# Local-plus-block attention and an MLP on one core: fewer early loads, key copies on chip, and a new order list

## The chip, the cores and the metric

The kernel runs on one core of one Trainium2 chip. The metric is the device time of one execution in microseconds, smaller being better. Names used below: PE is TensorE (matmuls and transposes), DVE is VectorE, ACT is ScalarE, POOL is GpSimd, SP is SyncE, which here only issues loads and stores. SBUF is the on-chip memory of 128 rows, PSUM the memory into which PE writes.

## The reference

Four batches of eight heads, 768 tokens, head width 64. Each query sees the keys within 15 tokens of it, and beside them 24 summaries of the sequence, one for each block of 32 tokens: the key of a block is the maximum over its keys, its value the mean of its values. The attention output goes into a two-layer MLP with a rational activation. q, k and v are 32-bit, the weights come as 64-bit floats.

```python
k_sum = k.reshape(B, H, nb, block, D).max(axis=3)
v_sum = v.reshape(B, H, nb, block, D).mean(axis=3)
scores_l = scale * np.matmul(q, k.transpose(0, 1, 3, 2))
mask_l = np.abs(pos[:, None] - pos[None, :]) < window      # window = 16
scores_s = scale * np.einsum('bhsd,bhnd->bhsn', q, k_sum) + np.log(block)
scores_all = concat([where(mask_l, scores_l, -1e9), scores_s])
a = softmax(scores_all)
attn = a @ concat([v, v_sum])                              # 3072 tokens x 512
h = attn @ w_in                                            # 512 -> 2048
P = a[0] + a[1]*h + a[2]*h**2 + a[3]*h**3
Q = 1.0 + abs(b[0])*abs(h) + abs(b[1])*h**2
out = (P / (Q + 1e-6)) @ w_out                             # 2048 -> 512
```

## The kernel before

**Units of work.** The 3072 tokens are cut into 48 "halves" of 64 queries (`HQ`), 12 in a batch, all eight heads at once. A half needs 96 keys and values around its queries (`NKW`, 16 tokens of margin on either side) and the 24 block summaries, so 120 columns (`NK`). Eight halves make a group of 512 tokens, and there are six groups. For each group the MLP runs over 16 column blocks of 128 (`fc`), so 96 steps; a step n is written g_fc, h0_4 being step 4. In a step the first layer (`moe1`) gives h from x, which is kept as a high part xh and a rest xl; the activation (`gelu`, parts a to k) gives a high part gh and a rest gl; and the second layer (`moe2`) adds into four PSUM tiles po. Each layer takes three products of high parts and rests.

**A half.** PE writes the scores (sc), DVE adds the mask and finds the row's extreme (sm), ACT takes the exponentials with their sum, DVE the reciprocal, POOL or DVE scales (ss). PE then transposes the result into pt, ACT copies it to pts, PE multiplies by the values (av), ACT copies av to xh, and DVE takes av minus xh as xl.

**Halves 0 to 7** ("early") are the first group. Their keys lie in `kres`, the padded keys of the whole first batch (four loads K0 to K3), and their queries in `qres`; each half has a value tile of its own (`vres`: vw0, vw1, vr0 to vr3, vlast). From half 8 on `att_load` brings queries (qw) and windowed keys (kw) of a half into two alternating buffers. The block means of the values come from PE: `window_average` and `value_average` add up averaging products of the value tiles in one PSUM tile (vf), and `first_means` copies the result into rows 96 to 119 of each value tile. The second batch's means (vf1, `quarter_average`) are made likewise.

**Weights.** `w_load` brings one column block of both weights as 1 MB of 64-bit numbers (wr). `w_split` turns them into a high part and a rest: a Prelu over them on ACT (called a prelude here), a scaling of one byte plane on POOL, a shift on DVE, then a copy to the high part on ACT (a cast) and the rest on DVE.

**What sets the order.** Up to about step 13 a list written out by hand, `TEXT` (lines 48 to 59). `token` (line 683) turns each entry into instructions, and each engine issues its own in the order in which the list names them. A letter is a kind of work, the number a half, a block or a step: K and k load and reduce keys, Q loads queries, M loads constants, V and v load and average values, F and G load more values of the first two batches, m copies the means, h takes a half one stage on, A is `att_load`, W and w load and split weights, x and y are the layers, g with a letter a part of the activation. Z is a spare matmul of the mask against the identity whose result nobody reads; `FILL` puts one such matmul ahead of half 8's transposes. The steps behind the list are ordered by a scheduler from a loop (lines 752 to 786), which the change leaves alone.

**PSUM.** Eight buffers: four (`ps_o`) for early scores and later po, two (`ps_h`) for h, for early pt and for the spares, two (`ps_a`) for vf, av and the scores and pt of halves 8 and up.

All engine instructions go through one wrapper, so the profile gives them all line 114; they are told apart by their tiles' names. In the order rows a name carries a running number, and wearly, w8 and so on are finished weights.

## Time and profile before

| | |
|---|---|
| times of three runs | 629.84 (median), 628.6, 635.0 us |
| the profiled execution | 629.4 us |
| its span in the trace | 627.5 us |
| mean granted clock of PE | 0.997 of full speed |
| PE busy | 615.8 us, 98% of the span |
| DVE, ACT, POOL busy | 558.9, 458.8, 261.4 us |

The span runs from the first to the last instruction of the trace; the 1.9 us that the execution took beyond it lie around it. Busy time is the time in which an engine worked on an instruction, waiting left out; PE's ends are modelled, since its matmuls overlap. An engine that is busy for 98% of the span leaves 11.7 us in which it did nothing.

### The profile page before, as it was taken

The numbers are of one execution on the slowest core, as the hardware profiler recorded it, in microseconds if no ns is written. First come the engines' busy times: TensorE is split into PE (matmuls) and PEld (weight loads), VectorE is DVE, ScalarE is ACT, GpSimd is POOL, SyncE is SP. The second block draws the span as 40 slices with busy tenths as digits, with TensorE's granted clock in tenths as the row PEclk, the third lists the DMA queues.
The fourth block names the chain that finished last, engine by engine and source line by source line (L and its number), as shares of the span: only waits on it lengthen the run. The fifth ranks groups of instructions, "written<-read, shape, count | busy, mean of one in ns | idle before, by whom it ended". The sixth has DMA issues, their size and how long they took to land.

```text
span 627.5 us, 11968 instructions
## 1 busy us (share of the span) xinstructions
PE 615.8 (98%) x4126; PEld 494.0 (79%) x4126; DVE 558.9 (89%) x1139; ACT 458.8 (73%) x1031; POOL 261.4 (42%) x351
## 2 busy tenths in 40 slices
PE   7989999999999999999999999999999999999997
PEld 4466777878888888888888888888888888888885
DVE  5889999999799999799999899888988988898885
ACT  3999999986866767866766867757767765755563
POOL 1587598725433435323334145334243242222221
PEclk9999999999999999999999999999999999999999
DMA  8989989232444444334434524224233120100001
GB/s 315 315 327 332 282 254 296 81 110 75 151 128 129 119 148 133 135 98 126 118 104 129 166 79 129 77 66 129 89 115 119 40 67 1 67 1 1 1 1 67
DMA packets 51444, 80.29 MB, mean 128 GB/s; under 512 B 6344, under 2 KB 32904, under 8 KB 49464
## 3 DMA queue, kind: packets, MB, share of 16 engines
q1 hardware_dynamic: 49672, 75.01, 36.6%
q0 software_dynamic: 1280, 4.39, 3.0%
q8 instruction: 32, 0.52, 0.3%
q14 instruction: 28, 0.23, 0.1%
q10 hardware_dynamic: 432, 0.13, 0.1%
HBM read 60.33 MB, written 14.75 MB: 120 GB/s over the span
## 4 chain that ended last, share of the span: by engine, by line
PE 90%; DMA 4%; ACT 2%; DVE 1%; POOL 1%; SPq 1%; issue 0%; ACTq 0%; POOLq 0%
PE po L114 42%; PE h L114 41%; PE av L114 4%; PE sc L114 3%; DMA wr<-in_wio_dram 2%; DMA vf<-in_vpad_dram 1%; DMA mask<-in_cmask_dram 1%; ACT ss L114 1%; POOL ss L114 1%; PE pt L114 1%; ACT wr L114 1%; SPq L114 1%; DVE wr L114 0%; ACT pts L114 0%; POOL wr L114 0%
## 5 line engine op out<-in xcount | busy, mean ns | idle before, releaser
L114 POOL TENSOR_TENSOR gl<-tu,ta 128x512 fp32r<-128x512 f32 x96 | 132.5, 1381 | 292.3 <-DVE tu L114 153.0
L114 PE MATMUL po<-wearly,gh 128*128 128x512 f32 x384 | 120.4, 395 | 0.0
L114 PE MATMUL po<-w,gh 128*128 128x512 f32 x384 | 119.7, 393 | 0.0
L114 ACT ACTIVATE ta<-tq,cs 128x512 f32<-128x512 f32 x96 | 69.7, 726 | 68.2 <-DVE tq L114 67.3
L114 POOL TENSOR_SCALAR ss<-ss,sm 128x120 f32<-128x120 f32 x176 | 85.3, 504 | 38.5 <-DVE sm L114 37.7
L114 PE MATMUL h<-xh,wearly 128*128 128x512 f32 x384 | 96.7, 392 | 0.1
L114 PE MATMUL h<-xh,w 128*128 128x512 f32 x384 | 96.7, 391 | 0.1
L114 PEld LDWEIGHTS h<-xh,wearly 128*128 128x128 f32 x384 | 71.6, 188 | 16.4 <-ACT pts L114 0.7
L114 PEld LDWEIGHTS h<-xh,w 128*128 128x128 f32 x384 | 71.8, 188 | 15.5 <-PE spare L114 0.6
L114 PEld LDWEIGHTS po<-wearly,gh 128*128 128x128 f32 x384 | 70.9, 188 | 16.1 <-issue 1.6
L114 PEld LDWEIGHTS po<-w,gh 128*128 128x128 f32 x384 | 71.3, 188 | 15.6 <-issue 1.1
L114 ACT ACTIVATE ss<-ss,sm 128x120 f32<-128x120 f32 x188 | 71.8, 386 | 13.7 <-DVE sm L114 13.7
L114 DVE SCALAR_TENSOR_TENSOR gh<-tu,cs,ta 128x512 fp32r<-128x512 f32 x96 | 74.2, 774 | 8.5 <-ACT ta L114 1.2
L114 DVE SCALAR_TENSOR_TENSOR tu<-tu,cs,tq 128x512 f32<-128x512 f32 x96 | 72.5, 755 | 2.9
L114 PE MATMUL po<-w,gl 128*128 128x512 f32 x192 | 74.9, 390 | 0.0
L114 PE MATMUL po<-wearly,gl 128*128 128x512 f32 x192 | 74.9, 390 | 0.0
L114 ACT ACTIVATE tu<-h,cs 128x512 f32<-128x512 f32 x96 | 74.6, 779 | 0.0
L114 DVE SCALAR_TENSOR_TENSOR tu<-tu,cs,h 128x512 f32<-128x512 f32 x96 | 71.4, 744 | 2.7
L114 DVE SCALAR_TENSOR_TENSOR tq<-tq,gh 128x512 f32<-128x512 f32 x96 | 67.4, 702 | 2.8
L114 ACT ACTIVATE ta<-h,cs 128x512 f32<-128x512 f32 x95 | 64.6, 679 | 0.5 <-POOL gl L114 0.2
L114 DVE TENSOR_TENSOR tu<-tu,h 128x512 f32<-128x512 f32 x96 | 64.9, 676 | 0.0
L114 ACT ACTIVATE ta<-ta 128x512 f32<-128x512 f32 x96 | 60.8, 633 | 2.5
(92 smaller groups left out, 905.1 us busy)
## 6 DMA issues: line engine op xcount, KB each, us to landing
wr<-in_wio_dram SPq DMA_DIRECT2D x15, 1024.0 KB, 6.8
cross<-tb SPq DMA_DIRECT2D x32, 256.0 KB, 2.0
vw<-in_vpad_dram SPq DMA_DIRECT2D x42, 192.0 KB, 3.4
kw<-in_kwin_dram SPq DMA_DIRECT2D x40, 192.0 KB, 3.8
pts<-cross SPq DMA_DIRECT2D x96, 64.0 KB, 2.0
out_dram<-o SPq DMA_DIRECT2D x23, 256.0 KB, 2.1
qw<-in_qw_dram SPq DMA_DIRECT2D x40, 128.0 KB, 3.0
kr<-in_kraw_dram SPq DMA_DIRECT2D x12, 384.0 KB, 8.4
```

The costliest lines, as they stand in the source:

```text
L114: out = getattr(self.engine, name)(*args, **kw)
```

## The change

1. The early halves' values load as 128 rows rather than 96. The last 32 rows are those that follow in memory; rows 96 to 119 are overwritten by the means before they are read.
2. The windowed keys of halves 8 to 11, which lie in the first batch, are no longer loaded. POOL copies them out of `kres` (token B), and `att_load` brings keys from the second batch on.
3. Masks (three of 120 columns), identity and averaging matrices came as three loads of 180, 64 and 139 KB. Now the middle mask, the identity and a narrower averaging matrix come as one load of 156 KB into a tile `both`, and POOL makes the masks of the first and last half of a batch from the middle one, by a copy and a memset each (token N).
4. The averaging products write only the 24 rows of PSUM that are used (`NKW:NK`) instead of 120, and the activation's coefficients are loaded straight into `cs`.
5. Spare matmuls have 312 columns instead of 360.
6. The list `TEXT` is new from the first entry to the last (583 entries instead of 578).

```diff
--- before.py
+++ after.py
@@ -45,20 +45,20 @@
-TEXT = ("K0 k0 K2 K1 S0 k1 k2 K3 k3 Q0 h2 h3 M0 h3 h3 h0 h1 h0 Q1 h3 h0 h0 h3 h3 h1 W0 M1 h3 Z4 F0 h2 h0 w0 w0 w0 h8 h3 h2 h1 h1 h1 h2 h6 h6 h6 h4 h5 h7 h7 h7 h0 V2 v2 w0 w0 h6 h14 v9 "
...
-AVGW = NK + NB - 8
-AVGH = NK + NB - 2
+TEXT = ("K2 K0 Q0 S0 k0 k2 K1 k1 K3 k3 B8 h8 M0 W0 h0 N0 h0 h2 Q1 h1 h1 h3 h0 h0 h0 w0 V2 F0 h3 h3 h1 h1 Z1 V3 V5 B9 h3 Z0 h6 h1 v2 w0 h7 h7 h7 h7 V6 h2 h3 h2 h2 v9 h4 h5 h0 w0 h7 w0 "
...
+AVGH = 40
+NCONST = NK + P + AVGH + NB
...
@@ -125,26 +125,24 @@
-    ident = const.tile([P, P], F32, name="ident")
-    mask = const.tile([P, 3, NK], F32, name="mask")
-    coef = const.tile([P, 6], F32, name="coef")
+    both = const.tile([P, NCONST + 2 * NK], F32, name="both")
+    mid, ident, avg = both[:, 0:NK], both[:, NK:NK + P], both[:, NK + P:NCONST]
+    ends = both[:, NCONST:].rearrange("p (m k) -> p m k", m=2)
...
-    vw = [const.tile([NK, DM], F32, name=f"vw{i}") for i in range(2)]
+    vw = [const.tile([P, DM], F32, name=f"vw{i}") for i in range(2)]
...
-    kfull = wm.tile([P, NPAIR * SPAD + AVGW + AVGH], F32, tag="wm", name="kres")
-    kres = kfull[:, 0:NPAIR * SPAD].rearrange("p (r s) -> p r s", r=NPAIR)
-    avg = kfull[:, NPAIR * SPAD:]
-    avgw = kfull[0:NKW, NPAIR * SPAD + AVGW:]
+    kfull = wm.tile([P, NPAIR * SPAD], F32, tag="wm", name="kres")
+    kres = kfull.rearrange("p (r s) -> p r s", r=NPAIR)
     def setup():
-        nc.scalar.dma_start(out=coef[:, 0:4], in_=a)
-        nc.scalar.dma_start(out=coef[:, 4:6], in_=b)
-        dve.tensor_scalar_mul(cs[:, 0:6], coef, SH)
+        nc.scalar.dma_start(out=cs[:, 0:4], in_=a)
+        nc.scalar.dma_start(out=cs[:, 4:6], in_=b)
+        dve.tensor_scalar_mul(cs[:, 0:6], cs[:, 0:6], SH)
...
@@ -204,11 +202,12 @@
     def value_average(kind, av, n, k, vt):
...
-        pe.matmul(av[:NK, :], avg[:, AVGW - NK - 8 * (k // 2):AVGW - 8 * (k // 2)], vt, start=(order[kind] == 1), stop=(order[kind] == n))
+        lo = NB - 8 - 8 * (k // 2)
+        pe.matmul(av[NKW:NK, :], avg[:, lo:lo + NB], vt, start=(order[kind] == 1), stop=(order[kind] == n))
     def quarter_average(av, n, k, vt):
...
-        lo = NKW + NB - 8 - 8 * (k // 2)
+        lo = NB - 8 - 8 * (k // 2)
...
@@ -216,7 +215,8 @@
     def window_average(av, n, jj):
...
-        pe.matmul(av[:NK, :], avgw[:, AVGH - NK - 2 * jj:AVGH - 2 * jj], vres[jj][0:NKW, :], start=(order["v"] == 1), stop=(order["v"] == n))
+        lo = AVGH - 2 * jj
+        pe.matmul(av[NKW:NK, :], avg[0:NKW, lo:lo + NB], vres[jj][0:NKW, :], start=(order["v"] == 1), stop=(order["v"] == n))
     def first_means(av):
...
@@ -241,7 +241,8 @@
...
-        syn.dma_start(out=kw[jj % 2][:, 0:NKC - 1], in_=kwin[bi, j])
+        if bi:
+            syn.dma_start(out=kw[jj % 2][:, 0:NKC - 1], in_=kwin[bi, j])
     def key_blocks(jj):
...
@@ -291,7 +292,7 @@
     def softmax(jj, sc):
...
-        mt = mask[:, 0 if j == 0 else (2 if j == NJ - 1 else 1), :]
+        mt = ends[:, 0, :] if j == 0 else ends[:, 1, :] if j == NJ - 1 else mid
...
@@ -360,7 +361,8 @@
...
-        syn.dma_start(out=vt[0:NKW, :], in_=vpad[bi, j * HQ:j * HQ + NKW, :])
+        rows = P if jj < HPG else NKW
+        syn.dma_start(out=vt[0:rows, :], in_=vpad[bi, j * HQ:j * HQ + rows, :])
...
@@ -374,7 +376,7 @@
     def turned(jj, early=False):
...
-            pe.matmul(pt[:, 0:3 * NK], ident, mask.rearrange("p m k -> p (m k)"), start=True, stop=True)
+            pe.matmul(pt[:, 0:NCONST], ident, both[:, 0:NCONST], start=True, stop=True)
...
@@ -649,8 +651,8 @@
...
-    vres = vw + [mp.tile([NK, DM], F32, tag=t, name=f"vr{i}") for i, t in enumerate(("ta", "tq", "ta", "tq"))]
-    vlast = stage.tile([NK, 2, DM], F32, tag="st", name="vlast")
+    vres = vw + [mp.tile([P, DM], F32, tag=t, name=f"vr{i}") for i, t in enumerate(("ta", "tq", "ta", "tq"))]
+    vlast = stage.tile([P, 2, DM], F32, tag="st", name="vlast")
...
@@ -712,11 +714,17 @@
...
         elif kind == "Z":
...
-            pe.matmul(spare[:, 0:3 * NK], ident, mask.rearrange("p m k -> p (m k)"), start=True, stop=True)
+            pe.matmul(spare[:, 0:NCONST], ident, both[:, 0:NCONST], start=True, stop=True)
         elif kind == "M":
-            syn.dma_start(out=(mask, ident)[n], in_=(cmask, cident)[n])
+            syn.dma_start(out=both[:, 0:NCONST], in_=cboth)
+        elif kind == "N":
+            gps.tensor_copy(ends[:, n, :], mid)
+            gps.memset(ends[:, n, (NKW - WIN) * n:(NKW - WIN) * n + WIN], -1e9 / SCALE)
+        elif kind == "B":
+            gps.tensor_copy(
+                kw[n % 2][:, 0:NKC - 1].rearrange("p c r n -> p r c n"),
+                kres[:, :, n * HQ:n * HQ + NKW].rearrange("p r (c n) -> p r c n", n=NB))
         elif kind == "F":
-            syn.dma_start(out=kfull[:, NPAIR * SPAD:], in_=cavg)
...
         elif kind == "G":
```

The first place is the start. SP's queue of loads; in its names both is the tile of constants, vlast, vr and vw are early halves' values, and wr0 and wr1 are weights. Before:

```order
L114 DMA kres_107<-in_kraw_dram 128x800 x4
L114 DMA qres_106<-in_qfirst_dram 128x1024
L114 DMA mask_96<-in_cmask_dram 128x360
L114 DMA qres_106<-in_qfirst_dram 128x1024
L114 DMA wr0_244<-in_wio_dram 128x2048
L114 DMA ident_95<-in_cident_dram 128x128
L114 DMA kres_107<-in_cavg_dram 128x278
L114 DMA vf0_0_255<-in_vpad_dram 128x1024
L114 DMA vr0_115<-in_vpad_dram 96x512
L114 DMA vlast_119<-in_vpad_dram 96x512
L114 DMA wr1_379<-in_wio_dram 128x2048
L114 DMA vlast_119<-in_vpad_dram 96x512
```

After:

```order
L114 DMA kres_105<-in_kraw_dram 128x800 x2
L114 DMA qres_104<-in_qfirst_dram 128x1024
L114 DMA kres_105<-in_kraw_dram 128x800 x2
L114 DMA both_95<-in_cboth_dram 128x312
L114 DMA wr0_146<-in_wio_dram 128x2048
L114 DMA qres_104<-in_qfirst_dram 128x1024
L114 DMA vr0_113<-in_vpad_dram 128x512
L114 DMA vf0_0_239<-in_vpad_dram 128x1024
L114 DMA vr1_114<-in_vpad_dram 128x512
```

All three kinds of constants now come in one row ahead of the first weight, a load of queries stands between the key loads, and the rows of kw are gone.

POOL's list at the start. ISA is the instruction that reloads POOL's function library, ss1 belongs to half 1, and wr0 is the first weight. Before:

```order
L114 ISA
L114 TENSOR_SCALAR wr0_244<-wr0_244 128x1024
L114 TENSOR_TENSOR ss1_238<-ss1_238,sm1_239 128x4x120
L114 TENSOR_SCALAR ss0_219<-ss0_219,sm0_220 128x120 x4
L114 TENSOR_SCALAR ss1_238<-ss1_238,sm1_239 128x120 x4
```

After:

```order
L114 COPY kw0_97<-kres_105 128x4x4x24
L114 COPY both_95<-both_95 128x120
L114 MEMSET both_95 128x16
L114 ISA
L114 TENSOR_TENSOR ss1_225<-ss1_225,sm1_226 128x4x120
L114 COPY kw1_98<-kres_105 128x4x4x24
L114 TENSOR_SCALAR wr0_146<-wr0_146 128x1024
```

A key copy and an end mask moved ahead of the library reload, and half 1's subtract (the TENSOR_TENSOR) moved ahead of the first weight.

The second place is the way to PE's first layer. On PE, from the last values of the early halves on (h0_0 is step 0, sc10 and sc11 are scores of halves 10 and 11). Before:

```order
L114 MATMUL av5_609<-pts5_521,vr3_118 64x64 x8
L114 MATMUL av1_620<-pts1_547,vw1_104 64x64 x8
L114 MATMUL av4_640<-pts4_489,vr2_117 64x64 x8
L114 MATMUL av6_652<-pts6_633,vlast_119 64x64 x8
L114 MATMUL spare1_671<-mask_96,ident_95 128x360
L114 MATMUL h0_0_682<-xh0_472,wearly_105 128x512 x8
L114 MATMUL h0_0_682<-xl0_473,wearly_105 128x512 x4
L114 MATMUL spare3_703<-mask_96,ident_95 128x360
L114 MATMUL sc10_707<-kw0_99,qw0_101 64x120 x2
```

After:

```order
L114 MATMUL av1_602<-pts1_475,vw1_102 64x64 x8
L114 MATMUL pt6_617<-both_95,ss6_382 120x128 x4
L114 MATMUL av5_629<-pts5_558,vr3_116 64x64 x8
L114 MATMUL av6_641<-pts6_622,vlast_117 64x64 x8
L114 MATMUL spare2_653<-both_95 128x312
L114 MATMUL h0_0_655<-xh0_477,wearly_103 128x512 x8
L114 MATMUL h0_0_655<-xl0_478,wearly_103 128x512 x4
L114 MATMUL sc10_697<-kw0_97,qw0_99 64x120 x2
L114 MATMUL sc11_698<-kw1_98,qw1_100 64x120 x2
```

The transposes of half 6 moved between the values of halves 1 and 5, and one spare behind h0_0 is gone.

On ACT, around the first xh cast (the rows of vw0 and vw1 are copies of the means). Before:

```order
L114 COPY pts0_445<-pt0_432 120x512
L114 COPY vw0_103<-vf_366 24x512
L114 COPY vw1_104<-vf_366 24x512
L114 COPY pts7_462<-pt7_457 120x512
L114 CAST xh0_472<-av0_474 128x4x64
L114 COPY pts4_489<-pt4_467 120x512
```

After:

```order
L114 COPY vw0_101<-vf_298 24x512
L114 COPY vw1_102<-vf_298 24x512
L114 COPY pts1_475<-pt1_396 120x512
L114 CAST xh0_477<-av0_479 128x4x64
L114 ACTIVATE wr2_458<-wr2_458 128x1024
L114 COPY pts4_495<-pt4_490 120x512
```

The xh cast that stood behind pts7 now stands right behind pts1.

The third place is step 4's activation on ACT (ta0_4, whose last two rows are its Ln and Exp; ss12 are half 12's exponentials, w8 a pass over weight 8). Before:

```order
L114 ACTIVATE wr10_972<-wr10_972 128x1024
L114 ACTIVATE ta0_5_1016<-tq0_5_1017,cs_98 128x512
L114 ACTIVATE ta0_5_1016<-ta0_5_1016 128x512
L114 ACTIVATE wr9_1037<-wr9_1037 128x1024
L114 ACTIVATE ta0_4_953<-tq0_4_954,cs_98 128x512
L114 ACTIVATE ta0_4_953<-ta0_4_953 128x512
L114 ACTIVATE ss12_1101,sm12_1102<-ss12_1101,sm12_1102 128x120 x4
L114 ACTIVATE sm12_1102<-sm12_1102 128x4
L114 COPY pts10_1138<-pt10_1112 120x512
L114 ACTIVATE w8_1094<-w8_1094 128x1024
```

After:

```order
L114 ACTIVATE wr15_0_1026<-wr15_0_1026 128x512
L114 ACTIVATE wr15_1_1027<-wr15_1_1027 128x512
L114 ACTIVATE ta0_5_1041<-tq0_5_1042,cs_96 128x512
L114 ACTIVATE ta0_5_1041<-ta0_5_1041 128x512
L114 ACTIVATE ss12_1091,sm12_1092<-ss12_1091,sm12_1092 128x120 x4
L114 ACTIVATE sm12_1092<-sm12_1092 128x4
L114 ACTIVATE w8_1052<-w8_1052 128x1024
L114 COPY pts11_1163<-pt11_1129 120x512
L114 ACTIVATE ta0_4_999<-tq0_4_1000,cs_96 128x512
L114 ACTIVATE ta0_4_999<-ta0_4_999 128x512
```

Step 4's Ln and Exp moved behind half 12's exponentials, the pass over weight 8 and the copies pts10 and pts11.

## Rows read from the trace of the kernel before

**Rows 1.** First part of the page: span, then busy time, share and instructions of each engine.

```profile
span 627.5 us, 11968 instructions
...
PE 615.8 (98%) x4126; PEld 494.0 (79%) x4126; DVE 558.9 (89%) x1139; ACT 458.8 (73%) x1031; POOL 261.4 (42%) x351
```

**Rows 2.** Windows: stretch, length, busy of PE, PEld, DVE, ACT, POOL, PEclk, DMA share, GB/s.

```profile
11.45:59.00 47.55, 41.17 (x508) 27.51 (x499) 41.77 (x145) 45.91 (x128) 32.71 (x44) 0.96 0.95 322
59.00:100.00 41.00, 40.94 (x263) 32.01 (x259) 40.47 (x71) 40.58 (x87) 29.62 (x30) 1.00 0.93 285
```

**Rows 3.** PE's waits, 14 to 57 us: waiter, what it waited for, total, times, longest.

```profile
PE pt L114 <- DVE ss L114: 2.1, 1, 2.1
PE av L114 <- DVE xl L114: 1.6, 2, 0.9
PE vf L114 <- DMA vr<-in_vpad_dram: 0.9, 1, 0.9
PE vf L114 <- DMA vf<-in_vpad_dram: 0.6, 1, 0.6
PE vf L114 <- DMA vw<-in_vpad_dram: 0.4, 1, 0.4
```

**Rows 4.** Timeline of PE: start, length, instructions; in brackets the wait ahead of them.

```profile
31.52 0.69 PE L114 MATMUL av<-pts,vw 120*64 120x64 f32 x16
32.61 0.65 PE L114 MATMUL pt<-ident,ss 128*120 128x128 f32 x4 [0.41 <-ACT pts L114]
...
43.32 2.11 PE L114 MATMUL h<-xh,wearly 128*128 128x512 f32 x8
...
50.72 0.77 PE L114 MATMUL pt<-mask,ident 128*128 128x360 f32 x2
...
88.03 0.63 PE L114 MATMUL po<-wearly,gh 128*128 128x512 f32 x2
```

**Rows 5.** Timeline of ACT: casts and preludes at 41.5 us; step 4's Exp and half 12.

```profile
41.50 1.22 ACT L114 CAST wearly<-wr 128x1024 fp32r<-128x1024 f32 x1
42.57 0.70 ACT L114 CAST xh<-av 128x256 fp32r<-128x256 f32 x2
43.10 1.22 ACT L114 ACTIVATE wr<-wr 128x1024 f32<-128x1024 f32 x1
...
79.48 0.64 ACT L114 ACTIVATE ta<-ta 128x512 f32<-128x512 f32 x1
80.02 0.38 ACT L114 ACTIVATE ss<-ss,sm 128x120 f32<-128x120 f32 x1
...
81.78 0.57 ACT L114 COPY pts<-pt 120x512 f32<-120x512 f32 x1
82.34 1.06 ACT L114 ACTIVATE w<-w 128x1024 fp32r<-128x1024 f32 x1
```

**Rows 6.** Windows of 1 us, PE alone: busy, PEclk, DMA share, GB/s.

```profile
20.00:21.00 1.00, 1.00 (x4) 1.00 1.02 205
...
35.00:36.00 1.00, 1.00 (x20) 1.00 1.07 431
```

**Rows 7.** Timeline of POOL: first operation, scalings of halves' rows, copies of the means.

```profile
13.79 1.43 POOL L114 TENSOR_SCALAR wr<-wr 128x1024 int32<-128x1024 uint8 x1 [13.34 <-DMA wr<-in_wio_dram]
...
18.89 1.38 POOL L114 TENSOR_SCALAR ss<-ss,sm 128x120 f32<-128x120 f32 x4 [0.16 <-DVE sm L114]
...
31.61 2.28 POOL L114 COPY vr<-vw 24x512 f32<-24x512 f32 x4 [1.77 <-ACT vw L114]
...
41.26 3.48 POOL L114 TENSOR_SCALAR ss<-ss,sm 128x120 f32<-128x120 f32 x4 [1.33 <-DVE sm L114]
```

**Rows 8.** Page part 5: busy and mean ns, then idle time ahead and its cause.

```profile
L114 POOL TENSOR_TENSOR gl<-tu,ta 128x512 fp32r<-128x512 f32 x96 | 132.5, 1381 | 292.3 <-DVE tu L114 153.0
...
L114 DVE SCALAR_TENSOR_TENSOR gh<-tu,cs,ta 128x512 fp32r<-128x512 f32 x96 | 74.2, 774 | 8.5 <-ACT ta L114 1.2
```

**Rows 9.** DMA queues, 0 to 13.8 us: packets, MB, share of time.

```profile
q1 hardware_dynamic: 1494, 4.35, 84.5%
```

More of the change, by code (lines that the diff above doesn't have):

```diff
@@ L85, in tile_kernel @@
 @with_exitstack
-def tile_kernel(ctx, tc, qfirst, qw_in, kraw, kwin, vpad, vred, wio, a, b, cmask, cident, cavg, out):
+def tile_kernel(ctx, tc, qfirst, qw_in, kraw, kwin, vpad, vred, wio, a, b, cboth, out):
     nc = tc.nc
@@ L401, in values @@
                     av[e * D:(e + 1) * D, pr * HQ:(pr + 1) * HQ],
-                    vt[:, (2 * pr + e) * D:(2 * pr + e + 1) * D],
+                    vt[0:NK, (2 * pr + e) * D:(2 * pr + e + 1) * D],
                     pts[:, pr, (e ^ turn) * HQ:((e ^ turn) + 1) * HQ], start=True, stop=True)
@@ L437, in both_values @@
                         av[e * D:(e + 1) * D, pr, k, :].rearrange("d (b q) -> d b q", q=SQ),
-                        vw[k][:, (2 * pr + e) * D:(2 * pr + e + 1) * D],
+                        vw[k][0:NK, (2 * pr + e) * D:(2 * pr + e + 1) * D],
                         pts[:, 2 * (e ^ k):2 * (e ^ k) + 2, pr, :], start=True, stop=True)
@@ L808, in _layout @@
     kr = np.arange(NKW)[None, :] - WIN
-    near = np.abs(qi - kr) < WIN
-    ms = []
-    for j in (0, 1, NJ - 1):
-        key = kr + j * HQ
-        ok = near & (key >= 0) & (key < S)
-        m = np.full((HQ, NK), math.log(BLK) / SCALE, f)
-        m[:, :NKW] = np.where(ok, 0.0, -1e9 / SCALE)
-        ms.append(np.concatenate([m, m], axis=0))
-    avg = np.zeros((P, AVGW + AVGH), f)
-    avg[np.arange(P), NKW + NB - 8 + np.arange(P) // 16] = 1.0 / BLK
+    near = np.where(np.abs(qi - kr) < WIN, 0.0, -1e9 / SCALE)
+    const = np.zeros((P, NCONST), f)
+    const[:, :NK] = math.log(BLK) / SCALE
+    const[:, :NKW] = np.concatenate([near, near], axis=0)
+    const[:, NK:NK + P] = np.eye(P)
+    avg = const[:, NK + P:]
+    avg[np.arange(P), NB - 8 + np.arange(P) // 16] = 1.0 / BLK
     rows = np.arange(HQ)
-    avg[WIN + rows, AVGW + NKW + NB - 2 + rows // BLK] = 1.0 / BLK
+    avg[WIN + rows, AVGH + rows // BLK] = 1.0 / BLK
     return {
@@ L824, in _layout @@
         "a": np.broadcast_to(moe_a.reshape(1, 4), (P, 4)), "b": np.broadcast_to(moe_b.reshape(1, 2), (P, 2)),
-        "cmask": np.stack(ms, axis=1).astype(f), "cident": np.eye(P, dtype=f), "cavg": avg,
+        "cboth": const,
     }
```

22 rows, old and new, of the table TEXT are left out of this document.

## The prediction, made before the changed kernel was run

> **What bounds the kernel now.** I read the page first. The span is 627.5 us and TensorE (PE) counts 615.8 us of it as busy [rows 1], so the most that can be won is the 11.7 us in which PE is idle and the matmuls that are mere filler. Next come the windows, to see where that idle time lies. From the first exponential at 11.45 us to 59 us PE is busy for 41.17 of 47.55 us; from 59 to 100 us for 40.94 of 41.00 [rows 2]. The reader should see two things in the second window: PE has no gap, and VectorE (DVE, 40.47) and ScalarE (ACT, 40.58) have next to none either. From 59 us on three engines are full at once. The instructions behind the order list are the same in both kernels, so the change can move the end in two ways only: PE's unbroken run starts earlier or later, or the new order tears a hole into it.
>
> Then PE's own waits between 14 and 57 us: seven, 6.0 us in all [rows 3], 0.41 of them in [rows 4]. 2.1 us are for the softmax of the first half, 1.9 us for loads (0.9, 0.6 and 0.4), 1.6 us for xl of earlier halves, 0.4 us for a pts copy. The rest of the 11.7 us is start, tail and gaps that this view doesn't name.
>
> But PE's early waits are not themselves the bound. In the first window ACT is busy for 45.91 of 47.55 us [rows 2]. The way into PE's first layer leads through ACT's queue: the last two xh casts stand at 42.57 us [rows 5], and the first h0_0 matmul at 43.32 [rows 4]. So what counts before h0_0 is how much work stands ahead of the last xh cast in ACT's queue, and how long ACT waits there.
>
> **Part by part.** *Order before h0_0.* ACT's list up to the last xh cast holds, before, nine softmaxes (halves 0 to 8), five weight preludes, four weight casts, and the copies of pts, means and xh. After, half 8's exponentials stand behind that cast, with one weight cast less and one prelude more ahead of it. A half's exponentials and sum take from 80.02 to 81.78, 1.76 us; a cast (41.50) and a prelude (43.10) of 1.22 us each cancel [rows 5]. That is -1.8 us. Against it stands a new wait: ACT's xh0 now follows pts1 directly, and av0 needs pt3, whose PSUM buffer only pts1 frees, so ACT waits through four transposes (0.65 at 32.61) and sixteen small matmuls (0.69 at 31.52) [rows 4], about 1.2 us since they overlap a little; before, pts7 filled that time. Sum -0.6 us. The ends are -1.8 (no wait) and +1.0 (another such wait on DVE, whose xl free the two buffers of these matmuls; the 1.6 us in rows 3 are its present size).
>
> *Start.* With K2, K0, Q0, K1, K3 in place of K0 to K3, Q0, the fourth key load comes after 512 KB more, and the last key sum ends up to 1 us later, near the end of the warm matmuls; I take 0.1 inside the term above. The scores of halves 6 and 7 can start about 3 us earlier, since the buffers of halves 0 and 1 come free first, and two spare matmuls fill the 2.1 us wait. I cost both at nothing, because ACT's queue covers them; without that cover they would be a gain of up to 2 us.
>
> *Fillers.* A spare matmul shrinks from 360 to 312 columns. The one at 50.72 is given as 0.77 us for its two passes [rows 4]; a column share of 48/360 of that is 0.10. Four stand inside PE's full run before (behind h0_0, the FILL of half 8, one behind it, one ahead of h0_8), and four after (that FILL, one ahead of h0_8, two further down). 4 x 0.10 less overlap is -0.3 us, ends -0.4 and +0.5, if one of the later ones takes a PSUM buffer that is wanted.
>
> *Loads.* Gone are four key windows of 192 KB and 227 KB of constants; added are 8 x 64 KB of values: 0.5 MB less in the queue. At 205 GB/s, the slowest microsecond among the value loads, and at the 431 of a weight load [rows 6] this is 2.4 or 1.2 us of queue time. What it can give the end is bounded by PE's waits for loads [rows 3]: 0.9 and 0.4 lie under ACT's queue, but the 0.6 us for the second batch's values lies in PE's run. These were queued behind weight 6, whose buffer came free late; now they stand ahead of weights 7 and 6. I take -0.6 us, ends -0.6 and 0. The 205 GB/s are 96-row loads and the 431 are loads of 128 rows, but those rows are also four times as long, so this trace doesn't say which of the two makes the rate. The Trainium skill, SBUF — State Buffer, "Door 1: The DMA port swizzle (why [64,N] ≈ [32,N])", says that bandwidth depends on how many of the 16 ports the partitions reach, and by its table partitions 0 to 95 put eight partitions on each even port and four on each odd one. By it a 128-row load would last no longer than a 96-row one, and the queue would win up to 2.5 us more; the sum would stay, as only the 0.6 us lie in PE's run.
>
> *Copies on GpSimd (POOL).* Four key copies of 128 x 384 and two mask copies with memsets are new. The nearest rows are a 24 x 512 copy (2.28 us for four, 0.57 each) and four scalings that cover 128 x 480 (1.38 us) [rows 7]: between 0.4 and 1.4 us each, and I take 0.8, nearer the copy. POOL is busy for 32.71 of the 47.55 us [rows 2], so its own free time hides them. Where they stand in a queue matters more (rivals).
>
> *Middle, 59 to 110 us.* By these terms PE comes 1.4 us earlier to step 4, which it asks for right behind h0_7: 86.6 us instead of 88.03 [rows 4]. Step 4's Exp ends at 80.1 us now. In the new list half 12's exponentials (1.76), a pass over weight 8 (1.06) and two pts copies (0.57 each) move ahead of it [rows 5]; weight 15's two preludes take the place of weight 10's. That makes it 4.0 us later, 84.1. From there to gl it takes three DVE steps of about 774 ns and one on POOL of 1381 [rows 8], 3.7 us, so gl comes at 87.8, 1.2 us after PE asks; gh is there earlier and covers 0.4 of it. I give back 0.8 us, ends 0 and 2.2, since DVE and ACT are full there and can't make up for a slip.
>
> The sum is -0.6 - 0.3 - 0.6 + 0.8 = -0.7 us. The profiled execution took 629.4 us (627.5 of span), so it would be 628.7; the median of the runs shown, 629.84, lies 0.44 above the profiled one, so the median becomes 629.1 us.
>
> **Rivals.** *Loads bind the start.* If loads and not ACT pace the first 57 us, all 6.0 us of PE's waits can go: 623.8. For it speaks that the DMA engines are busy for 0.95 of that window; against it, that ACT has only 1.6 us of idle time there [rows 2].
>
> *POOL's reload stands in the way (the slower side).* POOL's list holds one instruction that reloads its function library. Before, it stood first, ahead of an operation that began at 13.79 us after 13.34 of waiting [rows 7]. Now it stands behind two copies that wait for the keys and the mask (ready at about 10.5 us), and ahead of half 1's subtract, wanted at about 12.9. It decides from 2.4 us on: beyond that every microsecond goes into ACT's queue, where half 1's exponential stands near the head. The trace bounds its length by 0 and 13.3 us. In the first 13.8 us the kernel's loads are all that the queues moved [rows 9], so I take it as short. At 8 us it would cost 5.6: 634.7.
>
> *The middle takes back more.* POOL's copies for halves 10 and 11 fall between 35 and 42 us, where DVE writes the xl that PE waits for. Equal scalings on POOL took 1.38 and 3.48 us [rows 7], so the two engines do get into each other's way. If DVE stands still for two key copies and a mask copy (0.8 + 0.8 + 0.4 = 2 us), or step 4 costs its 2.2 us and one more slip like it follows, the end is 631 to 633. The Trainium skill, SBUF — State Buffer, "SBUF: two separate sides", calls the port pair of VectorE and GpSimd an exclusive lock in which the loser blocks for the whole instruction. By that rule the full 2 us would be lost, and the time would be 631.1.
>
> *Nothing reaches the end.* Every load saved was hidden and ACT keeps its pace: 629.8, inside my forecast.
>
> **How the numbers follow.** Forecast, 627.5 to 631: 0.55. Loads bind, 622 to 626: 0.15. The middle takes back more, 631 to 634: 0.18. Reload, 634 to 640: 0.07. Anything else, mostly a hole in the order that I haven't seen: 0.05. With some tenth left out on each side the range is 624.5 to 634. A measurement of this kernel can tell about 1% from no change, 6.3 us. Faster than 623.5 is half of the load rival, 0.08; slower than 636.1 is most of the reload and the unknown, 0.08; within, 0.84.
>
> **What would show it.** Right: h0_0 within 1 us of 43.3; a gap of about 1 us on ACT ahead of xh0; no wait of PE for the second batch's values; one short wait for step 4's gl between 85 and 92 us. Wrong: half 1's subtract on POOL later than 14 us (reload); h0_0 before 41 us (loads bound the start); several waits of PE between 60 and 140 us.

## Result and the profile after

| | before | after |
|---|---|---|
| median of the runs | 629.98 us (10 runs, 628.47 to 635.04) | 636.1 us (10 runs, 633.77 to 637.69) |
| ratio, 95% interval | | 1.0086 [1.0065, 1.0107] |
| profiled execution, its span | 629.4, 627.5 us | 633.77, 632.0 us |

The change costs 0.9%, 6.1 us of the median; forecast were 629.1 us and a range up to 634.0. The profiled execution of after is the fastest of its ten, so some 2 us of the median's loss are not in the trace shown here.

The page of after, span and first part:

```profile
span 632.0 us, 11971 instructions
PE 616.7 (98%) x4126; PEld 493.0 (78%) x4126; DVE 560.8 (89%) x1139; ACT 459.9 (73%) x1031; POOL 261.9 (41%) x359
```

Busy time is 0.9 us more on PE, the span 4.5 us [rows 1]: the engines do nearly the same work and stand still longer. The windows of after (columns as in rows 2), then SP's first output store on its timeline:

```profile
11.45:59.00 47.55, 40.51 (x477) 25.22 (x468) 39.40 (x137) 42.87 (x122) 29.43 (x44) 0.93 0.85 318
59.00:100.00 41.00, 38.37 (x259) 29.98 (x258) 38.62 (x69) 39.47 (x88) 33.20 (x33) 1.00 0.88 266
```

```profile
167.47 4.15 SPq L114 DMA_DIRECT2D out_dram<-o  x4
```

The same two stretches and the same store of before are in rows 2 and here:

```profile
163.25 4.13 SPq L114 DMA_DIRECT2D out_dram<-o  x4
```

4.2 of the 4.5 us are lost ahead of the first store, and the rest of the kernel takes as long as it did. Up to 100 us PE was idle for 7.9 us before and is for 11.1 now. Of these 3.2 us more, 2.6 lie in the second window. There, where three engines were full [rows 2], PE now has 2.6 us of gaps, DVE 2.4 and ACT 1.5; in the first, ACT did 3.0 and DVE 2.4 us less than before.

PE's waits in after, 14 to 57 us and then 57 to 100 (columns as in rows 3):

```profile
PE av L114 <- ACT vw L114: 2.3, 1, 2.3
PE h L114 <- ACT xh L114: 1.3, 1, 1.3
...
PE vf L114 <- DMA vf<-in_vpad_dram: 0.7, 1, 0.7
...
PE av L114 <- DMA vw<-in_vpad_dram: 2.6, 1, 2.6
PE h L114 <- DVE tu L114: 0.5, 1, 0.5
```

The three waits for loads of rows 3 are gone; the 0.7 us for vf here is another one, for the first batch's values at 15.9 us. From 14 to 57 us PE's waits add up to 6.0 us as before, but they lie elsewhere: it waits for the means (vw, copied by ACT) at 28.5 us and for xh ahead of h0_0. New behind 59 us is the wait for half 8's values. Timeline of PE in after:

```profile
30.79 1.12 PE L114 MATMUL av<-pts,vw 120*64 120x64 f32 x16 [2.26 <-ACT vw L114]
...
44.26 2.11 PE L114 MATMUL h<-xh,wearly 128*128 128x512 f32 x8 [1.26 <-ACT xh L114]
...
62.53 0.69 PE L114 MATMUL av<-pts,vw 120*64 120x64 f32 x16 [2.57 <-DMA vw<-in_vpad_dram]
```

So h0_0 comes 0.94 us later than in rows 4, not earlier. That is one execution of each: in four kernels of the experiments whose lists differ from after's up to that point in at most one load it comes between 43.33 and 44.32 us, and in three with the start of before between 42.90 and 43.41. Timeline of ACT, around the two places:

```profile
30.16 1.06 ACT L114 COPY vw<-vf 24x512 f32<-24x512 f32 x2
...
35.86 0.59 ACT L114 COPY pts<-pt 120x512 f32<-120x512 f32 x1 [0.49 <-PE pt L114]
37.03 0.38 ACT L114 CAST xh<-av 128x256 fp32r<-128x256 f32 x1 [0.58 <-PE av L114]
...
43.55 0.66 ACT L114 CAST xh<-av 128x256 fp32r<-128x256 f32 x2
...
59.40 1.06 ACT L114 ACTIVATE wearly<-wearly 128x1024 fp32r<-128x1024 f32 x1 [1.78 <-DMA wearly<-wr]
```

The last row is a multiplication for weight 5. Weights 5, 7 and 8 get their high part by a DMA that POOL issues, and ACT waits for it from 57.62 to 59.40 us, mostly ahead of the second window; in before's trace ACT has no wait for such a DMA up to 100 us. DVE's timeline has a third wait for a load near it:

```profile
63.32 0.95 DVE L114 TENSOR_REDUCE ks<-kr 128x24 f32<-128x768 f32 x1 [1.49 <-DMA kr<-in_kraw_dram]
```

SP's queue of loads says where these three come from (start, length, load):

```profile
39.60 3.09 SPq L114 DMA_DIRECT2D vf<-in_vpad_dram  x2
46.57 0.33 SPq L114 DMA_DIRECT2D kr<-in_kraw_dram  x1
47.73 2.60 SPq L114 DMA_DIRECT2D wr<-in_wio_dram  x3
50.38 0.55 SPq L114 DMA_DIRECT2D vw<-in_vpad_dram  x1
```

SP issues in order. From 42.7 to 46.6 us it stands at the key load I1, whose buffer DVE's key sums (ks) haven't freed yet; then three weights of 1 MB go out within 2.6 us, and half 8's values stand behind them. Before, the weights there went out singly:

```profile
41.22 0.37 SPq L114 DMA_DIRECT2D wr<-in_wio_dram  x1
48.45 0.33 SPq L114 DMA_DIRECT2D wr<-in_wio_dram  x1
```

### The profile page after: what moved, and what is told of

It reads as the page before. It is cut to its first block, busy times and chain, and to the rows that moved or that the text cites. A ratio compares the mean times of both kernels' runs of the same rounds, so it can differ in the third digit from the quotient of the medians.

```text
span 632.0 us, 11971 instructions
## 1 busy us (share of the span) xinstructions
PE 616.7 (98%) x4126; PEld 493.0 (78%) x4126; DVE 560.8 (89%) x1139; ACT 459.9 (73%) x1031; POOL 261.9 (41%) x359
## 4 chain that ended last, share of the span: by engine, by line
PE 91%; DMA 5%; DVE 2%; ACT 1%; POOL 1%; issue 0%; SPq 0%; ACTq 0%
PE po L114 42%; PE h L114 40%; PE av L114 4%; PE sc L114 3%; DMA vw<-in_vpad_dram 2%; DMA wr<-in_wio_dram 2%; DMA both<-in_cboth_dram 1%; PE pt L114 1%; DVE wr L114 1%; ACT ss L114 1%; DVE wearly L114 0%; SPq L114 0%; POOL ss L114 0%; PE spare L114 0%; DVE xl L114 0%
## 5 line engine op out<-in xcount | busy, mean ns | idle before, releaser
L114 POOL TENSOR_SCALAR ss<-ss,sm 128x120 f32<-128x120 f32 x176 | 83.4, 494 | 36.3 <-DVE sm L114 35.2
```

The lines of the kernel that those rows point to most:

```text
L114: out = getattr(self.engine, name)(*args, **kw)
```

## Experiments

All ratios are against before, with 95% intervals from runs on the same chip. Variants of the changed kernel ran on different chips, so they are compared by their ratios: after is at 1.0086 [1.0065, 1.0107]. Where an edit is of the order list, the diff shows the tokens around it, with semicolons between places.

**The parts without the list.** First the changed code under the old list, with the new tokens put where the loads had stood, and then where keys and buffers are surely ready:

```diff
-A9 A8 h8 ; A10 w2 ; A11 h10 ; M0 ; M1
+A9 B9 A8 B8 h8 ; A10 B10 w2 ; A11 B11 N1 h10 ; M0 N0 ; (none)
```

> The changed kernel's code (128-row values, key copies on POOL, one load of constants, 24-row averages, shorter spares) under the order list of before, with only the tokens for the copies added and those of the dropped loads removed. Theory (the list costs): the parts themselves cost nothing or gain a little, so the time is that of before or less, 628 to 630.5, and the 6 us come from the list. Rival (the parts cost): POOL's copies or the reload behind them slow the start, and the time stays above 633.

638.01 us, 1.0123 [1.0102, 1.0143]. PE waited for the key copies themselves: 1.94 and 3.13 us for kw. The trial was spoilt by its placing, so again:

```diff
-K3 k3 Q0 ; A10 w2 w2 ; M0 ; M1
+K3 k3 B8 B9 Q0 ; A10 w2 B10 B11 N1 w2 ; M0 N0 ; (none)
```

> The code of the changed kernel under the old list once more, with POOL's key copies put where they have time: those for halves 8 and 9 at about 10 us, ahead of POOL's first work, those for 10 and 11 and the last mask behind the byte scaling of weights 4 and 2. In e5 PE waited 5.1 us for two of them, which stood behind the copies of the means and behind half 8's scaling. The lists of ACT, DVE and PE are word for word those of before. Theory (the list costs, the parts don't): no wait of PE for a key copy, and 627.5 to 630.5 us, the time of before or a little less. Rival (the parts cost): 631.5 or more, with a wait that names its part.

629.43 us (12 runs, 628.96 to 630.42), 0.9982 [0.9963, 1.0001]. The lists of ACT, DVE and PE are those of before, and all parts of the change but the new list are in. They cost nothing that could be measured; the list costs the 6 to 7 us. Its windows, and its first store:

```profile
11.45:59.00 47.55, 40.34 (x499) 25.84 (x495) 41.87 (x147) 45.39 (x127) 34.57 (x47) 0.96 0.83 308
59.00:100.00 41.00, 40.94 (x276) 31.76 (x269) 39.25 (x71) 39.82 (x86) 27.28 (x29) 1.00 0.94 286
```

```profile
163.75 4.13 SPq L114 DMA_DIRECT2D out_dram<-o  x4
```

Then before with the wider value loads alone:

```diff
-syn.dma_start(out=vt[0:NKW, :], in_=vpad[bi, j * HQ:j * HQ + NKW, :])
+rows = P if jj < HPG else NKW
+syn.dma_start(out=vt[0:rows, :], in_=vpad[bi, j * HQ:j * HQ + rows, :])
```

> The kernel of before with one part of the change alone: the early halves' values load as 128 rows, 256 KB rather than 192 each. If the number of rows makes the rate, the queue moves about 400 GB/s from 20 to 28 us instead of 205 to 297, and the eight loads end no later than before although they move a third more; PE's two waits for them (0.9 and 0.4 us) shrink. If the rate lies in the rows' 2 KB, they last a third longer, some 2 us in all, and PE's waits for them grow. Either way ACT's queue paces the start, so the time stays within 1 us of 629.7.

628.61 us, 0.9973 [0.9952, 0.9994]: the lowest median of all kernels here. Of PE's two waits that were to shrink, the one for vw is gone, and the one for vr grew from 0.92 to 1.23 us.

**One repair of the new list at a time.** Half 8's values ahead of the weights:

```diff
-N1 w5 I2 ; gj1 V8 u3
+N1 w5 V8 I2 ; gj1 u3
```

> One token of the changed kernel's list is moved: half 8's values (192 KB) load ahead of the key loads and of weights 7, 6 and 8, when the queue stands nearly empty (34 to 39 us), rather than behind 3 MB of weights. Theory (queue): PE's 2.57 us wait for these values at 62.5 us is a loss of its own, and the time falls from 636.1 by 2.0 to 3.5 us, to 632.6 to 634.1; the wait is gone from the trace. Rival (full engines): DVE and ACT are busy for 38.6 and 39.5 of 41 us there and used the pause to catch up; the wait comes back as one for gl or xh, and the time stays within 1 us of 636.1.

634.97 us, 1.0072 [1.0051, 1.0092], not clear of after. The wait for the values is gone, and 4 us further on PE waits 1.86 us for the second batch's means (vn), which stand behind weight 5's multiplication in ACT's queue. Mostly as the rival had it.

Three spare matmuls ahead of half 3's transposes, to fill the gap at 28.5 us:

```diff
-FILL = "0000000010000000"
+FILL = "0003000010000000"
```

> The changed kernel with three spare matmuls ahead of half 3's transposes (FILL of half 3 is 3), where PE stands idle for 2.26 us from 28.5 us on and then works at half clock until 36.9 us. Theory (clock): without that pause the granted clock stays at 1.00 from 30 to 37 us, the transposes and values there take 0.65 to 0.7 us rather than 1.1, h0_0 starts 0.5 to 1.5 us earlier than 44.26, and the time falls by as much. Rival (ACT's queue): the copies and casts on ACT set the pace whatever PE's clock is, h0_0 stays within 0.3 us of 44.26 and the time within 0.5 of 636.1.

636.33 us, 1.0101 [1.0083, 1.0119]. From 30 to 37 us the granted clock now stays at 1.00 and h0_0 comes 1.66 us earlier, but half 8's values don't. Timeline of PE in this run, and its window of 59 to 100 us (PE alone, PEclk, DMA share, GB/s):

```profile
42.60 2.11 PE L114 MATMUL h<-xh,wearly 128*128 128x512 f32 x8 [0.79 <-ACT xh L114]
...
62.12 1.12 PE L114 MATMUL av<-pts,vw 120*64 120x64 f32 x16 [2.77 <-DMA vw<-in_vpad_dram]
```

```profile
59.00:100.00 41.00, 38.17 (x245) 0.92 0.82 243
```

All but 0.4 us of the gain at the start is waited away at 60 us. Then there is a second loss, which after doesn't have: from 60.5 to about 67 us, during this wait and behind it, the clock is at the lower of its two levels, while in after it is 1.00 in this window. So this run moved the stretch at the lower level rather than removing it, and is no clean test of what the filler is worth. The means ahead of half 5's exponentials did no more:

```diff
-w1 w1 h5 V7 ; m0 h5 h5 h3
+w1 w1 V7 ; m0 h5 h5 h5 h3
```

> The changed kernel with ACT's two copies of the means ahead of half 5's exponentials instead of behind them; nothing else moves on any engine. Theory (the means are late): the copies start at about 28.3 us instead of 30.16, PE waits for them 0.4 us rather than 2.26, its clock stays up, h0_0 comes 1 to 2 us earlier, and the time falls by 1 to 2 us. Rival (ACT's total work ahead of the last xh cast): the exponentials only stand later in the same queue, h0_0 moves by less than 0.5 us and the time by less than 0.5.

635.41 us, 1.0092 [1.0073, 1.011]. PE's wait for the means falls from 2.26 to 0.38 us, but it now waits 2.28 us, up to 31.74, for a pts copy, and h0_0 comes at 43.45.

Weight 6's load ahead of the key load at which SP stands:

```diff
-G0 u0 ; gf1 W6 h9
+G0 W6 u0 ; gf1 h9
```

> The changed kernel with one load moved: weight 6 is issued ahead of the key load that held the queue of loads until 46.57 us, at about 45 us, when its buffer is free, instead of behind weight 7 near 48 to 49. Theory (burst): the queue moved 98 to 174 GB/s from 46 to 48 us and then three weights at once; with 1 MB brought forward the burst ends about 2 us earlier, PE's wait for half 8's values shrinks from 2.57 us to under 1, ACT's wait for weight 5's DMA from 1.78 to under 1, and the time falls by 1.0 to 2.5 us. Rival (ACT and DVE are late on their own): the waits shrink, others take their place, and the time moves by less than 0.7.

634.1 us, 1.0055 [1.0023, 1.0088]. SP issues it at 44.98 instead of with the others. Timeline of PE in this run:

```profile
60.90 0.69 PE L114 MATMUL av<-pts,vw 120*64 120x64 f32 x16 [1.17 <-DMA vw<-in_vpad_dram]
```

PE's wait for the values falls to 1.17 us, and ACT's for weight 5 and DVE's for keys go, though 1.51 us of ACT for another load (wr) comes up. So the burst of weights makes these waits. It is worth the most of the single repairs, 2.0 us by the medians; but the interval overlaps that of after, so the size in time is not shown.

**Two cases that tell little.** Half 8's values early as above, and weight 5 made by a cast on ACT instead of POOL's DMA; the second kernel has the filler too:

```diff
-MODE = "ccccchchhceecccc"
+MODE = "ccccccchhceecccc"
```

> The kernel of e1 (half 8's values loaded early), in which weight 5 is split on ACT and DVE like weights 0 to 4 rather than by GpSimd's DMAs (mode c for h): it moves 1 MB of copies out of the burst of loads between 47 and 62 us, at one DVE subtraction of 1.2 us and a cast for a multiplication on ACT. Theory (burst): with three weights issued together behind 47.7 us, everything else that is loaded lands late; in e1 ACT still waited 1.81 us for that weight's DMA and PE then 1.86 us for ACT's copy of the second means. Both waits go, and the time falls by 1.5 to 3 us from e1's 635.0, to 632 to 633.5. Rival (ACT's and DVE's work): these engines are behind anyway, DVE gets 1.2 us more, and the time stays at 634.5 or above.

> The kernel of e7 with the three spare matmuls of e2 ahead of half 3's transposes. In e2 they brought h0_0 from 44.26 to 42.60 us, and the wait for half 8's values took that back. Theory (two losses in a row): with that wait gone the earlier start reaches the end, and the time is 1 to 1.7 us under e7's. Rival (loads and ACT set the time from 55 us on): the same as e7 within 0.5 us.

640.95 us, 1.0161 [1.0121, 1.0201], and 640.27 us, 1.0148 [1.011, 1.0185]. The cast came to stand ahead of half 8's exponentials and waited 2.77 us for DVE, and PE 4.85 us behind it. They show what one waiting instruction in a full queue costs, and nothing of the burst.

**Repairs together.** Values and filler:

> The changed kernel with e1's early load of half 8's values and e2's three spare matmuls, and nothing else (e7 and e8 added a cast that ACT had to wait for 2.77 us, and said nothing about the two). Theory (losses in a row): the start gained in e2, 1.66 us at h0_0, is no longer taken back by the wait for half 8's values, so the time lies 1.0 to 1.7 us under e1's, at 633.3 to 634. Rival (the loads pace everything from 50 us on): ACT waits for weight 5's DMA, which lands at the same moment as before, and the time stays within 0.5 us of e1's 635.0.

634.93 us, 1.0076 [1.0054, 1.0098]: no more than the values alone. With weight 6 too:

> All three edits in the changed kernel: half 8's values early, weight 6 early, three spare matmuls ahead of half 3's transposes. Theory (these three places hold most of the loss): 631 to 633, within 3 us of the kernel of before. Rival (the list is late in many places): 633.5 or more, with new waits of PE between 55 and 75 us.

637.2 us, 1.0102 [1.006, 1.0144]. Timeline of ACT in this run:

```profile
74.60 1.06 ACT L114 ACTIVATE wearly<-wearly 128x1024 fp32r<-128x1024 f32 x1 [2.72 <-DMA wearly<-wr]
```

That is weight 7: POOL issued its DMA at 66.23 us, SP a load of 1 MB at 66.37. Of only four executions one took 633.89 us, the others 636.8 to 638.3. The values early and weight 5's multiplication behind half 8's work:

```diff
-A13 i3 w5 w5 h10 ; h12 w8 gb2 ; h8 h8 gc2
+A13 i3 h10 ; h12 gb2 ; h8 h8 w5 w5 w8 gc2
```

> The kernel of e1 (half 8's values loaded early), in which ACT's multiplication that needs weight 5's DMA, with the DMA behind it, and the prelude of weight 8 stand behind step 2's first activations and half 8's xh cast, so that ACT need not stand for 1.8 us. Theory (ACT's and DVE's lost time sets the end): ACT's wait is gone, the copy of the second means comes 1 to 1.8 us earlier, and the time falls by 1 to 2 us from e1's 635.0, to 633 to 634. Rival (the moved DMA is then late for step 5, or the loads land late anyway): 634.6 or more, with a wait of ACT or PE further down.

637.18 us, 1.0106 [1.0053, 1.016]. The traced execution, at 641.49 us, is the slowest of the five. Weight 5's wait is gone; weight 7's is now 6.58 us at 78.42, its DMA issued at 68.83, behind a 1 MB load at 67.88. The values early and POOL's DMA for weight 7 right behind weight 5's:

```diff
-w5 w5 h10 ; w6 w7 h9 gf3
+w5 w5 w7 h10 ; w6 h9 gf3
```

> The kernel of e1 (half 8's values loaded early), in which GpSimd issues its DMA copy of weight 7 right behind weight 5's second DMA, at about 63 us, rather than behind two scalings at 66.7. Theory (a race of this copy with the loads of weights 9 and 15 sets the slow executions): ACT has no wait for it, the executions lie closer together, and the median falls by 1.5 to 3 us from e1's 635.0, to 632 to 633.5. Rival (the list is late for other reasons): 634.5 or more.

634.64 us, 1.0072 [1.0052, 1.0092]: there is no wait for weight 7, but the trace with the values alone had none either, and the time is the same. All four repairs (values, weight 6, filler, weight 7's DMA):

> e13's three edits (half 8's values early, weight 6 early, three spares ahead of half 3's transposes), which took 637.2 us with a wait of 2.72 us for weight 7's copy, together with e17's early issue of that copy. Theory (with the race gone the three edits bring what they promised): 631 to 633. Rival: 634.5 or more.

633.37 us, 1.0051 [1.0031, 1.0071]: by the medians 3.8 us less than the three without weight 7's DMA, and ACT's wait for weight 7 is gone. That speaks for the DMA as a cause where the other repairs have made the loads collide with it; with four executions on one side and overlapping intervals it isn't shown. PE still waited 2.33 us for vn. With vn ahead of half 8's cast as well:

```diff
-ge2 h8 h8 gc2 ; gf2 n0 w8
+ge2 n0 h8 h8 gc2 ; gf2 w8
```

> The kernel of e18 with one more instruction moved: ACT's copy of the second means (0.27 us) stands ahead of half 8's xh cast and weight 6's prelude, some 1.3 us earlier, and its store to memory with it. Theory (single places hold the loss): PE's wait of 2.33 us shrinks by about that, and the time falls by 0.8 to 1.5 us from e18's 633.4, to 632 to 632.6. Rival (backlog of ACT and DVE): the wait moves to gl or to h, and the time stays at 633 or above.

633.35 us, 1.0053 [1.0035, 1.007]. Timeline of PE in this run:

```profile
65.28 0.74 PE L114 MATMUL po<-wearly,gh 128*128 128x512 f32 x2 [0.94 <-ACT vn L114]
...
74.44 1.19 PE L114 MATMUL h<-xh,wearly 128*128 128x512 f32 x4 [0.89 <-DVE tu L114]
```

The wait shrinks by 1.4 us, a new one stands further on, and the median is the same.

**Damage done to before.** Ten ACT copies of 128x64 that nothing uses, behind step 2's Exp, and as a control the same ten in step 28:

```diff
+elif kind == "D":
+    for _ in range(10):
+        act.copy(dummy, dummy)
```

> The kernel of before with ten small extra copies on ACT (128 x 64 of a tile that nobody else uses, some 2 us together by the 0.20 us of a 128 x 4 operation in the profile) behind step 2's Exp at about 61 us, where PE, DVE and ACT are all full. Theory (ACT binds together with PE): the time rises by about what they take, 1.2 to 2.4 us. Rival (PE alone binds, ACT has a reserve in its buffers): within 0.6 us of before.

> The control: the same ten copies, here reading step 28's Exp, at about 200 us, where ACT is busy for some 70% of the time. Both theories: within 0.6 us of before.

2.4 us of ACT work at 60.9 us cost 1.6 us by the ratio (632.19, 1.0026 [0.9999, 1.0053]), at 224 us nothing (630.47, 1.0003 [0.9972, 1.0035]). PE's idle time between 59 and 100 us grew from 0.06 to 0.95. The two intervals overlap, and the first just holds no change at all: this supports that ACT's time counts in that stretch and doesn't prove it. Last, POOL's DMA for weight 7 put 10 us later in before:

```diff
-u2 w7 gi2 ; W10 gi3
+u2 gi2 ; W10 w7 gi3
```

> The kernel of before with one instruction moved: GpSimd issues its copy of weight 7 behind weight 8's scaling, at about 68.4 us instead of 58.8, a microsecond ahead of the load of weight 10. Nothing else changes its place on any engine. Theory (this place of the new list is worth several us): ACT, which needs the copy at 70.06 us, waits 4 to 7 us for it, and the time rises by 3 to 6 us, to 633 to 636. Rival (PE and the buffers absorb it): within 1.5 us of before.

630.8 us, 1.0021 [0.9997, 1.0046]; ACT waited 1.12 us for it. By the interval the late DMA is worth at most 2.9 us in before, and perhaps nothing; the 3 to 6 us of the theory are out.

## Why the prediction was wrong

**What is shown.** The parts cost nothing that could be measured, and the list costs all: 0.9982 [0.9963, 1.0001] under the old list, 1.0086 [1.0065, 1.0107] under the new one. In the trace of after the largest piece is the 2.57 us that PE stands for half 8's values, in a stretch where before had no gap. The burst of weights behind the key load makes this wait, ACT's 1.78 us for weight 5 and DVE's 1.49 us for keys: with weight 6 out of it they are 1.17 us and nothing. What the burst costs at the end is less sure, since the intervals of 1.0086 and 1.0055 overlap. All four repairs together bring 0.35 of the 0.86% back.

**What stays open.** The other 0.51%, 3.2 us. After most of the repairs a wait came up elsewhere. And even the part that came back has another reading, since executions of one kernel differ in PE's mean granted clock and with it in time. Before took 629.06 us (median) in those 30 of its 111 executions beside the experiments that had a mean clock of 0.999 or more, and 631.80 in the 27 below 0.996. Of after's ten, eight lie below 0.996 and none above 0.997; of the ten with four repairs, eight lie at 0.999 or more, and their median is 633.38 us. So at the same clock the four repairs are still 4.3 us over before, and after's two executions at 0.996 and 0.997 (634.45 and 634.58) are 4.7 over before's 629.77 at 0.996 to 0.998. What the repairs bring back is by this mostly a clock that stays up, and hardly any of the rest. The lower clock stands behind waits of PE in the traces, so the two come together, and no run changed the clock alone.

A reading that would fit the rest is that the new list leaves ACT and DVE with less done. Windows of 0 to 100 us (columns as in rows 2), of before, after, the parts under the old list, weight 6 early, and the four repairs:

```profile
0.00:100.00 100.00, 92.10 (x861) 64.53 (x862) 87.02 (x226) 87.78 (x215) 62.53 (x76) 0.98 0.93 305
```

```profile
0.00:100.00 100.00, 88.87 (x860) 60.62 (x861) 83.60 (x221) 84.10 (x212) 63.68 (x83) 0.97 0.86 295
```

```profile
0.00:100.00 100.00, 91.23 (x859) 62.53 (x860) 85.81 (x225) 86.50 (x213) 63.41 (x83) 0.98 0.87 298
```

```profile
0.00:100.00 100.00, 89.23 (x863) 60.36 (x864) 83.92 (x222) 84.84 (x212) 62.11 (x83) 0.98 0.86 298
```

```profile
0.00:100.00 100.00, 89.24 (x860) 60.05 (x861) 85.13 (x220) 83.65 (x210) 60.95 (x83) 0.98 0.84 291
```

DVE and ACT are 3.4 and 3.7 us behind in after, and the first store 4.2; 1.2 and 1.3 behind under the old list, the store 0.5; 3.1 and 2.9 with weight 6 early, the store (at 166.74) 3.5; 1.9 and 4.1 with the four repairs, the store (at 168.48, in the slowest of their ten executions) 5.2. ACT follows the store more closely than DVE does. This is a comparison of single executions, not a test, and an engine can also be behind because PE is; which rows of the list keep the engines idle for the rest was not settled.

**By the prediction's steps.**

- *Loads (-0.6, ends -0.6 and 0)* is the step that failed, as far as the runs show one. It followed what the move puts ahead of the weights, the second batch's values, and that was right: their 0.61 us in PE's run are gone. It gave no cost to what the move leaves behind the weights: half 8's values, the keys, and a DMA of POOL that shares the time with them. Nor did it see that SP would stand at I1 for 3.9 us first. The runs show, in place of an upper end of 0, a wait of 2.57 us on PE at 60 us, 1.78 on ACT and 1.49 on DVE. In after's trace that makes the term about +2; weight 6's run says 2.0 as well, but within its noise. The rest of the loss, 3 us or more, is tied by no run to a step of the prediction, and its cause stays open.
- *Order before h0_0 (-0.6)* measured +0.94 in the traced pair, inside its ends and with the wrong sign; the executions above spread from about 0 to +1. The gap of "about 1 us on ACT ahead of xh0" is there, 0.49 and 0.58 us. Left out was that the means' copies now stand behind half 5's exponentials, so that PE waits 2.26 us for them. At the end no gain from this term was seen: with the gap filled h0_0 came 1.66 us earlier and the time stayed, and with half 8's values early as well 1.0076 stands against 1.0072 for the values alone.
- *The accounting.* The prediction read that from 59 us on three engines are full, and then priced only PE's waits. Whether idle time of ACT and DVE there is made up isn't shown. The ten copies on ACT suggest that it isn't; but under the old list ACT stood idle for 1.2 us and DVE for 1.8 in this window, against 0.4 and 0.5 before, and the time was that of before.
- *Copies on POOL (0.8 each, hidden).* Right: the key copies take 0.50, the mask copies 0.29 us. PE never waited for one in the new list, and did in the trial with the copies placed late.
- *Rivals.* POOL's reload is out, since half 1's subtract begins at 12.44 us, as DVE's sm lands. Loads as the bound of the start are out for the new list, where h0_0 came no earlier; under the old one it came 0.7 us earlier with the wider loads, in a pair of single executions that also differ in PE's clock. "The middle takes back more" had the place and the sign, but neither of its mechanisms. Step 4's gl, forecast for 87.8 us, was ready at 91.88 and caused no wait, as PE came to it only at 92.48. And where POOL's copies overlap DVE's xl, the pair took 0.89 us, against 0.75 for the next pair and 0.76 for one before the change (the last row):

```profile
38.64 0.50 POOL L114 COPY kw<-kres 128x384 f32<-128x384 f32 x1
39.08 0.29 POOL L114 COPY both<-both 128x120 f32<-128x120 f32 x1
```

```profile
38.65 0.89 DVE L114 TENSOR_TENSOR xl<-av,xh 128x256 fp32r<-128x256 f32 x2
40.60 0.75 DVE L114 TENSOR_TENSOR xl<-av,xh 128x256 fp32r<-128x256 f32 x2
```

```profile
37.23 0.76 DVE L114 TENSOR_TENSOR xl<-av,xh 128x256 fp32r<-128x256 f32 x2
```

  That is 0.14 us beside copies of 0.50 and 0.29, not the 2 us of the prediction. The exclusive lock of the Trainium skill, SBUF — State Buffer, "SBUF: two separate sides", holds by that section only for a DVE operation with two inputs in SBUF or in a mode that uses both ports. The operation xl reads av from PSUM, so the prediction applied the rule where its condition of two SBUF inputs isn't met, and this pair doesn't test it.
- *Fillers (-0.3).* In PE's full run a spare took 0.69 us at 96.14 us, against 0.77 before the change [rows 4], near the forecast 0.10 less. The one at 53.19 us, behind a wait, took 0.76. The term was not tested alone.
- "Several waits of PE between 60 and 140 us" was named as what would prove it wrong, and "a hole in the order that I haven't seen" was most of a chance of 0.05. The trace of after has one such wait, not several, the 2.57 us. That case, and none of those worked out, is what the traces show.

## What to carry to other kernels

When an order list moves a load forward, write down for each queue what now stands behind it, DMAs of other engines that run at the same time among it, and at which load the queue will stand still. Once several engines are full, a sum has a column for each of them, and an idle microsecond on any of them is a candidate for the end, to be tested. When a repair seems to help, compare executions at the same granted clock before its wait is called the cause. Run the parts under the old order before the new order is judged: here the wider loads alone were a gain of 0.27% [0.06, 0.48], which the new list hid.

## What was new about the hardware

**Wide loads.** Here a load of 128 rows lasts no longer than one of 96. Windows of 20 to 28 us (PE alone, PEclk, DMA share, GB/s) of before and of before with the wider loads, while values are loaded:

```profile
20.00:28.00 8.00, 7.08 (x21) 1.00 1.04 286
```

```profile
20.00:28.00 8.00, 6.77 (x20) 1.00 1.05 399
```

The share is the same and 40% more goes through per microsecond. The one load of vr in this stretch whose landing the traces give landed 9.0 us behind its issue instead of 10.2. h0_0 came at 42.63 us instead of 43.32 [rows 4], but not by the loads alone: PE's clock, in before at its lower level from 14 to 17 us, was 1.00 there in this execution. The rate agrees with what the prediction worked out from the port table of the Trainium skill, SBUF — State Buffer, "Door 1: The DMA port swizzle (why [64,N] ≈ [32,N])".

**The clock.** Window of 30 to 37 us in after (PE alone):

```profile
30.00:37.00 7.00, 6.17 (x73) 0.51 0.60 220
```

Right behind PE's 2.26 us of waiting the granted clock is at the lower of its two levels, and stays there while PE is busy for 6.17 of 7 us; with the gap filled by spares it is 1.00. Not every such wait does it: behind the 2.57 us at 60 us in the same execution it stays at 1.00, and in the kernel with the spares it is at the lower level behind 2.77 us there.

**A DMA of POOL beside loads of SP.** The same DMA for weight 7 caused no wait where it was issued 0.7 us or more ahead of SP's loads of 1 MB (66.11 against 66.82, 66.19 against 66.97, 66.70 against 68.58 us), and 2.7 to 6.6 us on ACT where it was issued 0.1 us ahead or 0.95 behind (66.23 against 66.37, 68.83 against 67.88). The two kernels with the cast fit: 1.2 and 1.3 us behind, and waits of 2.83 and 2.94. In before, issued 10 us late but still 1.1 us ahead of the load, it cost 1.12. Each is one execution, and the runs don't say why so little decides.
